# An attention block and two expert layers on one core: the sum's transpose one unit later, the value product in one burst, half of the first weights' low parts on VectorE

## The chip, the cores and the metric

The kernel runs on one core of one Trainium2 chip. The metric is the device time of one execution in microseconds (us). Three runs of the kernel before took 1083.71 us in the median (1083.61 to 1087.17). The engines are TensorE (PE in the profile, PEld for its weight loads), VectorE (DVE), ScalarE (ACT), GpSimd (POOL) and SyncE (SP), which issues most of the DMAs.

## The reference

Three layers follow one another. The whole work is in float32.

```
scores = scale * q @ k.T + bias            # (4 batches, 8 heads, 576, 576); bias = relu(psi w1 + b1) w2, from positions
attn   = exp(scores - max); attn /= sum    # softmax over the last axis
x      = attn @ v                          # -> 2304 tokens x 512
h      = x @ w_in                          # 512 -> 2048
x      = (P(h) / Q(h)) @ w_out             # rational function, 2048 -> 512
h      = max(x @ w1, x @ w2, x @ w3)       # 512 -> 768
out    = h @ w_out2                        # 768 -> 512
```

## The kernel before

**Precision.** A float32 operand of a large product is split into a high part (a rounded cast) and a low part (the rest), and three products of such parts are summed. For the weights of the first expert layer (`wi`, sixteen tiles of 128x512) ScalarE casts the high part (L407) and GpSimd subtracts to get the low part (L408). Which engine subtracts is chosen by `low_eng` from a key of the table `KN`: `LOI` 0 means GpSimd for all of `wi`. The weights come as 64-bit values; ScalarE and VectorE narrow them (L382, L383, L391) in small steps `p1` and `p2` between ticks 9 and 70 of the attention, and SP stores and reloads them.

**Attention.** The work is cut into 80 units: a batch, a pair of heads `p`, and a block `t` of 128 query rows (`t` = 4 has 64 rows of both heads). From the second half of the first batch on, a pair of heads is two groups: rows blocks 0 and 1 (call the units A0, A1), then 2, 3 and 4 (B0, B1, B2). `attn_tick(n)` does for unit n the scores on TensorE (`sc`), the subtraction of the minimum with bias on VectorE (`r0`, `r1`, one for each head, L258) and the exponential on ScalarE (`e0`, `e1`). The sum of the exponentials comes with them. For unit n-1 it does `normalise` (`n`): GpSimd adds a small constant, VectorE takes the reciprocal (L270), GpSimd spreads it to a 128x128 tile `rb` (L272). For unit n-2 it does `T`: TensorE transposes the exponentials in eight pieces into two PSUM banks `tp`, then the last 128 columns into the left part of a bank `tt` (L302), then `rb` into its right part (L303). `v0` and `v1` copy the `tp` banks to `at` (on ScalarE; the second in turn on VectorE and ScalarE) and the whole `tt` to `att` (two of three times VectorE, else ScalarE).

**Value product.** When the last unit of a group has been transposed, `av` multiplies the transposed weights with the values (L338), in pieces over the next ticks: a group of two units takes 3 and 2 of its five column blocks `j`, a group of three 2, 2 and 1. One piece is taken in each tick. When the last is done, `st` multiplies by the transposed reciprocal (L344, VectorE) and SP stores the result.

**Order.** The steps stand in the list `A1` for the first 8 ticks, in `A2` after. In the ticks 8 to 79 the queues of SP, TensorE and VectorE follow the list; a planner at build time orders ScalarE and GpSimd. PSUM has eight banks: two pairs (`wide`, two buffers) for the scores and four single ones (`bank`) for `tp`, `tt`, `av` and others. From tick 61 on `weights_tick` runs at the end of each tick: load, narrow and split, one stage per tick and weight.

**The end of attention.** After unit 79 the ticks 80 to 84 still run `T` and the pieces of `av`, and with each of them one `ffn_tick` of the first expert layer, all in the planner's order on all engines but SP. From `ffn_tick` 5 on every engine follows the list order. An `ffn_tick` is twelve products for `ph`, twelve for `y` and the rational function on VectorE and ScalarE.

Of the kernel before, what the change touches and what calls it, by code (L numbers as in the profile page):

```python
# [17 lines left out]
P = 128  # L18
# [8 lines left out]
HID = 32  # L27
TOFF = 572
TW = 1148
KN = {'NSLOT': 35, 'NRAW': 3, 'NRAWX': 2, 'NATT': 4, 'HB': 0, 'NE': 'd', 'FP': 2, 'BL': 4, 'T4': 0, 'LSP': 1, 'KX': 4, 'HT': 'ss', 'EVP': 'da', 'TTP': 'dda', 'NXS': 4, 'EARLY': 0, 'NM0': 8, 'MAN': 2, 'MANF': 3, 'A1': ['b', 'T', 'sc', 'st', 'r0', 'av', 'b', 'b', 'b', 'sq', 'n', 'r1', 'p2', 'v0', 'v1', 'e0', 'e1'], 'A2': ['sc', 'av', 'p1', 'T', 'r1', 'r0', 'n', 'st', 'p2', 'sq', 'e0', 'e1', 'v0', 'v1'], 'LL': 10, 'SL': 4, 'LL0': 9, 'SL0': 4, 'SQ': [2, 1, 1], 'CUT2': 2, 'CUT3': 3, 'WS': 9, 'WE': 70, 'WT': 61, 'XT': 8, 'XA': 3, 'XB': 8, 'F': ['g2a', 'g2d', 'h', 'g1a', 'w', 'g2p', 'g1d', 'g1p', 'y', 'x', 'g3'], 'LOW': 4, 'LOM': 3, 'LOI': 0, 'GHI': 'dve', 'GLO': 'dve', 'BED': 8, 'BE0': 16, 'NU1': 'pool', 'XE': ['act', 'pool'], 'WR': 1, 'YSP': 'act', 'LAG': 2, 'EV1': 'dve', 'XSE': 'act', 'STQ': 'sp', 'PUQ': 'sp', 'NB0': 0, 'HP': 0, 'SB': 2, 'XLA': 3, 'XLB': 6, 'XSA': 11, 'YL': 10, 'YS': 14, 'WLOW': 1}  # L30
REBIAS = 2.0 ** -112
TOSIGN = -2.0 ** 32
QC = 1.0 + 1e-6
# [4 lines left out]
def tile_attention_moe(  # L38
# [7 lines left out]
    pe, act, dve, pool, sp = nc.tensor, nc.scalar, nc.vector, nc.gpsimd, nc.sync  # L46
# [17 lines left out]
    def big(name, shape, dt=F32):  # L64
        return sb.tile(shape, dt, tag="big", name=name, bufs=2)
# [4 lines left out]
    def bank(name):  # L70
        return ps.tile([P, 512], F32, tag="bank", name=name, bufs=4)
# [25 lines left out]
    A0, A1, A2, A3 = (par[:, i:i + 1] for i in range(4))  # L97
# [65 lines left out]
    def bias_hidden(t, g):  # L163
        hs = []
        for c in range(4):
            if c % 2 == 0:
                ht = {"r": raw, "x": rawx, "s": slot, "b": lambda *a: big(*a)}[KN["HT"][c // 2]](f"h{t}_{g}_{c}", [P, 2, S], F32)
            i0 = t * P + g * 16 + c * 4
# [110 lines left out]
    at = {}  # L279
# [4 lines left out]
        for n, t in enumerate(ts):  # L284
            at[b, t, p] = a, a2, n * P

    def transposes(b, t, p):
        et, st = ex.pop((b, t, p))
        a, a2, off = at[b, t, p]
        nu = 2 if t < 4 else 1  # L290
        flat = et.rearrange("p u j -> p (u j)")
        evac = []
        for u in range(nu):
            tp = bank(f"tp{b}_{t}_{p}_{u}")
            for j in range(4):
                pe.transpose(tp[:, j * P:(j + 1) * P], flat[:, 640 * u + j * P:640 * u + (j + 1) * P], ident)  # L296
            if t < 4:
                evac.append((a[:, :, u, off:off + P], tp.rearrange("p (j i) -> p j i", j=4)))
            else:
                evac.append((a[:, :, :, off:off + 64], tp.rearrange("p (j u i) -> p j u i", j=4, u=2)))  # L300
        tt = bank(f"tt{b}_{t}_{p}")
        pe.transpose(tt[:, :P], flat[:, 512:640], ident)  # L302
        pe.transpose(tt[:, P:2 * P], rbs.pop((b, t, p)).rearrange("p u d -> p (u d)"), ident)  # L303
        tr = tt[:, :2 * P].rearrange("p (w i) -> p w i", w=2)
        if t < 4:
            evac.append((a2[:, :, off:off + P], tr))
        else:
            for u in range(2):
                r = slice(64 * u, 64 * u + 64)
                evac.append((a2[r, :, off:off + 64], tr[r, :, r]))  # L310
        return evac

    def evac(e, pair):
        if e == "a":
            act.copy(*pair)
        elif e == "d":
            dve.tensor_copy(*pair)
        else:
            pool.tensor_copy(*pair)
# [257 lines left out]
    units = []  # L577
# [9 lines left out]
    NU = len(units)  # L587
# [117 lines left out]
    avq, stq = [], []  # L705
# [8 lines left out]
    def attn_tick(n):  # L714
        for t, p in bloads_at.get(n, []):
            if (t, p) not in bias:
                bias_load(t, p)
        for b, p in loads_at.get(n, []):
            if p % 2 == 0:
                load_v(b, p)  # L720
            load_kq(b, p)
        u0 = units[n] if n < NU else None
        u1 = units[n - 1] if 1 <= n <= NU else None
        u2 = units[n - KN["LAG"]] if KN["LAG"] <= n < NU + KN["LAG"] else None
        ev = []
        for step in KN["A1" if n < KN["NM0"] else "A2"]:
            if step == "sc" and u0:
                if u0[2] == u0[1][0]:
                    at_tiles(u0[0], u0[1], u0[3])
                scores(u0[0], u0[2], u0[3])  # L730
            elif step in ("r0", "r1") and u0:
                reduce_min(u0[0], u0[2], u0[3], int(step[1]))
            elif step in ("e0", "e1") and u0 and (step == "e0" or u0[2] < 4):
                expo(u0[0], u0[2], u0[3], int(step[1]))
            elif step == "st":
                while stq:
                    attn_store(*stq.pop(0))
            elif step == "T" and u2:
                ev = transposes(u2[0], u2[2], u2[3])
            elif step == "n" and u1:  # L740
                normalise(u1[0], u1[2], u1[3])
            elif step == "v0" and u2:
                act.copy(*ev[0])  # L743
            elif step == "v1" and u2:
                for e_ in ev[1:len(ev) - 1]:
                    evac(KN["EVP"][n % len(KN["EVP"])], e_)
                evac(KN["TTP"][n % len(KN["TTP"])], ev[-1])
            elif step == "b":
                bias_step()
            elif step in ("p1", "p2"):  # L750
                early_pop(n, 0.5 * int(step[1]))
            elif step == "av":
                if avq:
                    av, js = avq.pop(0)
                    attn_v(*av, js)
                    if 4 in js:
                        stq.append(av)
                if u2 and u2[2] == u2[1][-1]:
                    av = (u2[0], u2[1], u2[3])
                    cuts = {1: (5,), 2: (3, 2), 3: (2, 2, 1)}  # L760
                    cut = {1: (5,), 2: cuts[KN["CUT2"]], 3: cuts[KN["CUT3"]]}[len(u2[1])]
                    avq.extend((av, range(sum(cut[:k]), sum(cut[:k + 1]))) for k in range(len(cut)))
            elif step == "sq":
                for bp in splits_at.get(n, []):
                    sqq.extend(split_kq(*bp))
                for _ in range(2 if n < 10 else KN["SQ"][n % len(KN["SQ"])]):
                    if sqq:
                        sqq.pop(0)()
        WT, XT = KN["WT"], KN["XT"]
        if n == WT:  # L770
            todo.extend((slim["wi"], "wi", f, True, low_eng(KN["LOI"], f)) for f in range(NF))
        if n >= WT:
            weights_tick(KN["WR"])
        if n == NU - XT:
            load_x("x", x_d, 0, 0)
            load_x("x", x_d, 0, 1)
            todo.extend(wo_todo(f) for f in range(NF))
        for m, kcs in ((KN["XA"], (0, 1)), (KN["XB"], (2, 3))):
            if n == NU - XT + m:
                for kc in kcs:  # L780
                    split_x("x", 0, kc)
# [8 lines left out]
        for n in range(KN["NM0"], NU):  # L790
            attn_tick(n)
    n = NU
    while avq or stq or n < NU + KN['LAG']:
        attn_tick(n)
        ffn_tick(n - NU)
        n += 1
# [93 lines left out]
```

## Time and profile before

| | |
|---|---|
| median of three runs | 1083.71 us |
| the profiled execution | 1085.02 us |
| its span, first to last instruction | 1083.2 us |
| TensorE busy, mean granted clock | 1034.7 us (96%), 0.982 |
| VectorE / ScalarE / GpSimd busy | 657.7 / 622.8 / 452.7 us |
| scores, value product, transposes of `e` (L233, L338, L296) on TensorE | 86.4, 79.0 + 23.8, 81.5 us |

Busy time of TensorE is modelled at its ends and consecutive matmuls overlap, so a busy TensorE is read by its successive starts. The attention takes about the first 363 us; the first expert layer follows up to about 780 us, the second to the end. "Granted clock" 1.00 is TensorE's full speed (2.4 GHz), 0.5 its lower level (1.2 GHz).

### The profile page before, as it was taken

To read this page: it belongs to the slowest core of one execution; us is meant where nothing else is said; L and a number is where in the kernel's file an instruction comes from. 1 tells how busy PE (TensorE), PEld (TensorE's weight loads), DVE (VectorE), ACT (ScalarE), POOL (GpSimd) and SP (SyncE) were. 2 spreads that over 40 slices of the span, in tenths; PEclk is the share of its full clock that TensorE was granted. 3 is DMA by queue.
4 is the path that set the end of the run, shared out by engine and by line. 5 is a ranking of instruction groups with operands and counts; after the bars stand their busy time and mean duration, and the time that the engine had idled before them with its cause. 6 is when DMAs were issued, how large, how long until landed. Compare 5 with 4: busy or idle time off the path is not lost. (4 is left out here: it accounts for less than half of the span.)

```text
span 1083.2 us, 16519 instructions
## 1 busy us (share of the span) xinstructions
PE 1034.7 (96%) x5996; PEld 814.2 (75%) x5996; DVE 657.7 (61%) x1296; ACT 622.8 (57%) x1226; POOL 452.7 (42%) x569
## 2 busy tenths in 40 slices
PE   5689899999998889999999999999999999999998
PEld 2247777777765668878889888788888888888887
DVE  8485667676665789777779877799954211111111
ACT  5685676776776878676678766788733211211111
POOL 7605767677696534332233322333533330211111
PEclk9799999999998889999999999999999999999999
DMA  7486854454453442010020200034243200201010
GB/s 266 138 298 216 294 182 151 158 190 158 157 184 123 147 142 78 1 59 1 0 79 1 79 1 0 24 114 136 84 142 105 78 1 1 78 1 59 1 40 20
DMA packets 43394, 107.94 MB, mean 100 GB/s; under 512 B 4784, under 2 KB 11184, under 8 KB 43312
## 3 DMA queue, kind: packets, MB, share of 16 engines
q1 hardware_dynamic: 38128, 96.27, 26.8%
q10 hardware_dynamic: 5184, 10.62, 2.5%
q8 instruction: 47, 0.77, 0.3%
q14 instruction: 35, 0.29, 0.1%
HBM read 77.90 MB, written 28.97 MB: 99 GB/s over the span
## 5 line engine op out<-in xcount | busy, mean ns | idle before, releaser
L454 PE MATMUL p<-ys,wm 128*128 128x512 f32 (+1 forms) x1080 | 227.0, 368 | 0.0
L454 PE MATMUL ph<-xs,wwi 128*128 128x512 f32 (+1 forms) x960 | 215.9, 373 | 3.5 <-ACT at L743 2.6
L454 PEld LDWEIGHTS p<-ys,wm 128*128 128x128 f32 x1080 | 188.9, 188 | 34.3
L454 PE MATMUL y<-gs,wwo 128*128 128x512 f32 (+1 forms) x905 | 204.4, 373 | 1.3 <-POOL gs L502 1.1
L454 PEld LDWEIGHTS ph<-xs,wwi 128*128 128x128 f32 x960 | 169.7, 190 | 38.4 <-POOL xs L446 3.0
L502 POOL TENSOR_TENSOR gs<-g,gs 128x512 fp32r<-128x512 f32 (+1 forms) x80 | 96.1, 1201 | 237.2 <-ACT gs L501 170.2
L454 PEld LDWEIGHTS y<-gs,wwo 128*128 128x128 f32 x905 | 158.4, 188 | 34.5 <-POOL gs L502 2.4
L264 ACT ACTIVATE e<-e,st 128x576 f32<-128x576 f32 x144 | 111.1, 772 | 61.2 <-DVE st L258 44.3
L258 DVE CUSTOM_DVE_ANT_0 e<-s,bias 128x576 f32<-128x576 f32 x144 | 104.3, 754 | 44.9 <-PE s L233 32.4
L546 POOL TENSOR_TENSOR h2s<-mx,h2s 128x512 fp32r<-128x512 f32 (+1 forms) x30 | 35.5, 1183 | 225.5 <-ACT h2s L545 225.5
L542 DVE TENSOR_TENSOR mx<-p,mx 128x512 f32<-128x512 f32 (+1 forms) x30 | 19.1, 637 | 141.4 <-PE p L454 137.5
L475 ACT ACTIVATE s<-ph,keep 128x512 f32<-128x512 f32 (+1 forms) x80 | 49.5, 618 | 90.3 <-PE ph L454 89.9
L545 ACT CAST h2s<-mx 128x512 fp32r<-128x512 f32 (+1 forms) x30 | 17.3, 578 | 127.8 <-DVE mx L543 127.8
L296 PEld LDWEIGHTS tp<-ident,e 128*128 128x128 f32 x576 | 62.1, 141 | 35.7 <-issue 20.1
L233 PE MATMUL s<-k,qs 128*128 128x288 f32 x512 | 86.4, 309 | 2.2 <-ACT bo L194 1.5
L296 PE MATMUL tp<-ident,e 128*128 128x128 f32 x576 | 81.5, 281 | 1.2 <-ACT at L743 1.2
L477 DVE SCALAR_TENSOR_TENSOR g<-g,keep,s 128x512 f32<-128x512 f32 (+1 forms) x80 | 55.3, 692 | 41.5 <-ACT g L476 40.4
L338 PE MATMUL av<-at,v 128*64 128x320 f32 (+3 forms) x576 | 79.0, 396 | 0.0
L560 PE MATMUL o<-wmo,h2s 128*128 128x512 f32 x324 | 78.6, 390 | 0.0
L233 PEld LDWEIGHTS s<-k,qs 128*128 128x128 f32 x512 | 71.3, 191 | 5.6 <-issue 2.6
L185 PE MATMUL pb<-h,keep 128*32 128x288 f32 x576 | 49.2, 450 | 24.1 <-ACT h L173 23.2
L560 PEld LDWEIGHTS o<-wmo,h2s 128*128 128x128 f32 x324 | 60.4, 188 | 12.6 <-POOL h2s L546 0.4
(98 smaller groups left out, 1599.6 us busy)
## 6 DMA issues: line engine op xcount, KB each, us to landing
bias_d<-bo ACTq DMA_DIRECT2D x36, 288.0 KB, 3.1
kr<-in_k SPq DMA_DIRECT2D x16, 576.0 KB, 4.3
qr<-in_q SPq DMA_DIRECT2D x16, 576.0 KB, 4.3
bias<-bias_d SPq DMA_DIRECT2D x16, 576.0 KB, 5.5
wrm<-in_m SPq DMA_DIRECT2D x18, 512.0 KB, 3.6
wrwin<-in_wi SPq DMA_DIRECT2D x16, 512.0 KB, 5.4
wrwo<-in_wo SPq DMA_DIRECT2D x16, 512.0 KB, 3.6
v<-in_v SPq DMA_DIRECT2D x8, 576.0 KB, 4.3
```

The source lines that it names most:

```text
L185: pe.matmul(pb[32 * c:32 * c + 32, x, :HS], lhsT=hw_sb, rhs=hs[c][:, x * HS:(x + 1) * HS], start=True, stop=True,)
L233: pe.matmul(pt[:, x, :HS], lhsT=qs[:, u, t * P:(t + 1) * P], rhs=ks[u][:, w, x * HS:(x + 1) * HS], start=w == 0, stop=w == 1,)
L258: dve.tensor_tensor_reduce(out=dst, in0=src, in1=bs, op0=ALU.add, op1=ALU.min, scale=-0.125, scalar=3.0e38, accum_out=st[:, u:u + 1],)
L264: act.activation(et[:, u], et[:, u], AF.Exp, bias=st[:, u:u + 1], scale=-1.0, accum_out=st[:, 2 + u:3 + u])
L296: pe.transpose(tp[:, j * P:(j + 1) * P], flat[:, 640 * u + j * P:640 * u + (j + 1) * P], ident)
L338: pe.matmul(po[r, :n], lhsT=l, rhs=m, start=j == 0, stop=j == 4, skip_group_check=True)
L454: pe.matmul(po, lhsT=wpart(key, a, k), rhs=rhs, start=first and i == 0, stop=last and i == 2)
L475: act.activation(s, ph, AF.Abs, scale=B0)
L477: dve.scalar_tensor_tensor(q, q, B1, s, ALU.mult, ALU.add)
L502: pool.tensor_tensor(t[1], u, f32(t[0]), ALU.subtract)
L546: pool.tensor_tensor(t[:, 1], m, f32(t[:, 0]), ALU.subtract)
L560: pe.matmul(po, lhsT=h[:, a, tt * P:(tt + 1) * P], rhs=w[c], start=j == 0 and i == 0, stop=j == NF2 - 1 and i == 2,)
```

## The change

The table entries, the order lists and four places in the code change:

```diff
- 'A1': ['b', 'T', 'sc', 'st', 'r0', 'av', ...
+ 'A1': ['b', 'rb', 'T', 'sc', 'rv', 'st', 'r0', 'av', ...
- 'A2': ['sc', 'av', 'p1', 'T', 'r1', 'r0', 'n', 'st', 'p2', 'sq', 'e0', 'e1', 'v0', 'v1']
+ 'A2': ['sc', 'rb', 'av', 'p1', 'T', 'r0', 'r1', 'n', 'rv', 'st', 'p2', 'sq', 'e0', 'e1', 'v0', 'v1']
- 'CUT2': 2, 'CUT3': 3,   'LOI': 0
+                         'LOI': 2
-        tt = bank(f"tt{b}_{t}_{p}")
         pe.transpose(tt[:, :P], flat[:, 512:640], ident)
-        pe.transpose(tt[:, P:2 * P], rbs.pop((b, t, p)).rearrange("p u d -> p (u d)"), ident)
-        tr = tt[:, :2 * P].rearrange("p (w i) -> p w i", w=2)
...
+        evac.append(rows(b, t, p, 0, tt[:, :P]))
+    def rows(b, t, p, w, tr):
+        _, a2, off = at[b, t, p]
+        if t < 4:
+            return [(a2[:, w, off:off + P], tr)]
+        return [(a2[r, w, off:off + 64], tr[r, r]) for r in (slice(0, 64), slice(64, P))]
+    def transpose_sum(b, t, p, tt):
         pe.transpose(tt[:, P:2 * P], rbs.pop((b, t, p)).rearrange("p u d -> p (u d)"), ident)
+        return rows(b, t, p, 1, tt[:, P:2 * P])
...
+        u3 = units[n - KN["LAG"] - 1] if KN["LAG"] < n <= NU + KN["LAG"] else None
+            elif step == "rb" and (u2 or u3):
+                tt = bank(f"tt{n}")
+                if u3:
+                    sums = transpose_sum(u3[0], u3[2], u3[3], tt)
+            elif step == "rv" and u3:
+                for e_ in sums:
+                    evac("d", e_)
             elif step == "T" and u2:
-                ev = transposes(u2[0], u2[2], u2[3])
+                ev = transposes(u2[0], u2[2], u2[3], tt)
...
-                    av = (u2[0], u2[1], u2[3])
-                    cuts = {1: (5,), 2: (3, 2), 3: (2, 2, 1)}
-                    cut = {1: (5,), 2: cuts[KN["CUT2"]], 3: cuts[KN["CUT3"]]}[len(u2[1])]
-                    avq.extend((av, range(sum(cut[:k]), sum(cut[:k + 1]))) for k in range(len(cut)))
+                    avq.append(((u2[0], u2[1], u2[3]), range(5)))
...
-    while avq or stq or n < NU + KN['LAG']:
+    while avq or stq or n <= NU + KN['LAG']:
```

`rb` is transposed for unit n-3, right behind the scores of unit n, into the right part of a bank `tt` that is taken anew in each tick; the left part of the same bank takes the last columns of unit n-2 in `T`. The two parts are copied apart: the sums by `rv` on VectorE, behind `n`, the columns in `v1` as before. `av` of a group runs whole in the tick after its last `T`. `r0` stands ahead of `r1`. With `LOI` 2, `low_eng` gives the odd ones of the sixteen `wi` tiles to VectorE. The attention ends with tick 82 in place of 84, so `ffn_tick` 3 and 4 leave the planned part.

## Rows read from the trace of the kernel before

**Rows 1.** Busy us of each engine, granted clock (PEclk), DMA in stages of 100 us.
```profile
200.00:300.00 100.00, 99.98 (x738) 74.33 (x737) 69.74 (x195) 72.28 (x170) 70.84 (x129) 1.00 0.51 169
300.00:400.00 100.00, 87.88 (x520) 63.17 (x520) 67.27 (x151) 74.28 (x159) 66.57 (x89) 0.90 0.51 157
```
**Rows 2.** What TensorE waited for: us in total, times, longest us.
```profile
PE tt L303 <- POOL rb L272: 8.8, 4, 4.7
PE y L454 <- ACT gs L501: 2.8, 1, 2.8
PE ph L454 <- ACT at L743: 2.6, 1, 2.6
```
**Rows 3.** Stages of 10 us, columns as in Rows 1: PE, PEld, DVE, ACT, POOL, clock.
```profile
320.00:330.00 10.00, 5.32 (x41) 3.67 (x38) 3.83 (x13) 5.98 (x16) 9.61 (x16) 0.91 0.24 69
330.00:340.00 10.00, 10.00 (x58) 7.17 (x57) 4.49 (x13) 5.33 (x14) 5.09 (x9) 0.75 0.57 184
370.00:380.00 10.00, 9.82 (x37) 6.18 (x38) 8.78 (x15) 7.46 (x15) 3.08 (x3) 0.70 0.52 166
390.00:400.00 10.00, 9.96 (x30) 7.56 (x31) 7.79 (x13) 6.95 (x12) 5.29 (x4) 0.68 0.48 164
```
**Rows 4.** Around the longest of those waits, in order of time: start us, us, engine.
```profile
323.83 0.16 DVE L270 RECIPROCAL st<-st 128x1 f32<-128x1 f32 x1 [2.94 <-POOL st L269]
...
329.36 0.29 POOL L272 COPY rb<-st 128x128 f32<-128x128 f32 x1
```
**Rows 5.** GpSimd's low parts of the first weights: busy, mean ns, idle before.
```profile
L408 POOL TENSOR_TENSOR wwi<-wrwi,wwi 128x512 fp32r<-128x512 f32 x15 | 19.3, 1291 | 6.9 <-ACT wwi L407 6.8
```
**Rows 6.** TensorE in order of time, an undisturbed stretch: start us, us.
```profile
335.72 1.29 PE L233 MATMUL s<-k,qs 128*128 128x288 f32 x8
336.94 1.30 PE L338 MATMUL av<-at,v 128*64 128x320 f32 x8
338.17 1.10 PE L296 MATMUL tp<-ident,e 128*128 128x128 f32 x8
...
339.24 1.53 PE L243 MATMUL s<-k,qtail 128*128 128x512 f32 x8
340.70 0.76 PE L338 MATMUL av<-att,v 64*64 64x320 f32 x4
341.39 1.09 PE L296 MATMUL tp<-ident,e 128*128 128x128 f32 x8
```
**Rows 7.** The value product of a group of two: in pieces, and once whole.
```profile
343.69 1.51 PE L338 MATMUL av<-at,v 128*64 128x256 f32 x12
...
347.43 0.65 PE L338 MATMUL av<-at,v 128*64 128x256 f32 x4
...
359.66 1.95 PE L338 MATMUL av<-at,v 128*64 128x256 f32 x16
```
**Rows 8.** VectorE in order of time: the two reductions of one unit.
```profile
337.05 0.76 DVE L258 CUSTOM_DVE_ANT_0 e<-s,bias 128x576 f32<-128x576 f32 x1 [0.24 <-PE s L233]
...
337.73 0.75 DVE L258 CUSTOM_DVE_ANT_0 e<-s,bias 128x576 f32<-128x576 f32 x1
```
**Rows 9.** VectorE by line and shape: busy us, mean ns, idle before.
```profile
L317 DVE COPY at<-tp 128x512 f32<-128x512 f32 x32 | 22.0, 687 | 12.0 <-PE tp L296 11.4
L317 DVE COPY att<-tt 128x256 f32<-128x256 f32 x42 | 17.6, 419 | 17.7 <-PE tt L303 17.6
...
L383 DVE TENSOR_SCALAR wrwin<-wrwin 128x512 int32<-128x512 int32 x16 | 13.0, 813 | 0.0
...
L344 DVE TENSOR_TENSOR xs<-av,att 128x320 f32<-128x320 f32 x14 | 6.6, 472 | 0.0
L408 DVE TENSOR_TENSOR wm<-wrm,wm 128x512 fp32r<-128x512 f32 x6 | 6.5, 1086 | 1.9 <-ACT wm L407 1.9
...
L317 DVE COPY att<-tt 64x128 f32<-64x128 f32 x19 | 5.5, 288 | 7.6 <-ACT att L315 5.0 <-PE tt L303 2.0
...
L408 DVE TENSOR_TENSOR wwo<-wrwo,wwo 128x512 fp32r<-128x512 f32 x4 | 2.7, 681 | 0.0
```

More of the change, by code (lines that the diff above doesn't have):

```diff
@@ L29 @@
 TW = 1148
-KN = {'NSLOT': 35, 'NRAW': 3, 'NRAWX': 2, 'NATT': 4, 'HB': 0, 'NE': 'd', 'FP': 2, 'BL': 4, 'T4': 0, 'LSP': 1, 'KX': 4, 'HT': 'ss', 'EVP': 'da', 'TTP': 'dda', 'NXS': 4, 'EARLY': 0, 'NM0': 8, 'MAN': 2, 'MANF': 3, 'A1': ['b', 'T', 'sc', 'st', 'r0', 'av', 'b', 'b', 'b', 'sq', 'n', 'r1', 'p2', 'v0', 'v1', 'e0', 'e1'], 'A2': ['sc', 'av', 'p1', 'T', 'r1', 'r0', 'n', 'st', 'p2', 'sq', 'e0', 'e1', 'v0', 'v1'], 'LL': 10, 'SL': 4, 'LL0': 9, 'SL0': 4, 'SQ': [2, 1, 1], 'CUT2': 2, 'CUT3': 3, 'WS': 9, 'WE': 70, 'WT': 61, 'XT': 8, 'XA': 3, 'XB': 8, 'F': ['g2a', 'g2d', 'h', 'g1a', 'w', 'g2p', 'g1d', 'g1p', 'y', 'x', 'g3'], 'LOW': 4, 'LOM': 3, 'LOI': 0, 'GHI': 'dve', 'GLO': 'dve', 'BED': 8, 'BE0': 16, 'NU1': 'pool', 'XE': ['act', 'pool'], 'WR': 1, 'YSP': 'act', 'LAG': 2, 'EV1': 'dve', 'XSE': 'act', 'STQ': 'sp', 'PUQ': 'sp', 'NB0': 0, 'HP': 0, 'SB': 2, 'XLA': 3, 'XLB': 6, 'XSA': 11, 'YL': 10, 'YS': 14, 'WLOW': 1}
+KN = {'NSLOT': 35, 'NRAW': 3, 'NRAWX': 2, 'NATT': 4, 'HB': 0, 'NE': 'd', 'FP': 2, 'BL': 4, 'T4': 0, 'LSP': 1, 'KX': 4, 'HT': 'ss', 'EVP': 'da', 'TTP': 'dda', 'NXS': 4, 'EARLY': 0, 'NM0': 8, 'MAN': 2, 'MANF': 3, 'A1': ['b', 'rb', 'T', 'sc', 'rv', 'st', 'r0', 'av', 'b', 'b', 'b', 'sq', 'n', 'r1', 'p2', 'v0', 'v1', 'e0', 'e1'], 'A2': ['sc', 'rb', 'av', 'p1', 'T', 'r0', 'r1', 'n', 'rv', 'st', 'p2', 'sq', 'e0', 'e1', 'v0', 'v1'], 'LL': 10, 'SL': 4, 'LL0': 9, 'SL0': 4, 'SQ': [2, 1, 1], 'WS': 9, 'WE': 70, 'WT': 61, 'XT': 8, 'XA': 3, 'XB': 8, 'F': ['g2a', 'g2d', 'h', 'g1a', 'w', 'g2p', 'g1d', 'g1p', 'y', 'x', 'g3'], 'LOW': 4, 'LOM': 3, 'LOI': 2, 'GHI': 'dve', 'GLO': 'dve', 'BED': 8, 'BE0': 16, 'NU1': 'pool', 'XE': ['act', 'pool'], 'WR': 1, 'YSP': 'act', 'LAG': 2, 'EV1': 'dve', 'XSE': 'act', 'STQ': 'sp', 'PUQ': 'sp', 'NB0': 0, 'HP': 0, 'SB': 2, 'XLA': 3, 'XLB': 6, 'XSA': 11, 'YL': 10, 'YS': 14, 'WLOW': 1}
 REBIAS = 2.0 ** -112
@@ L285, in at_tiles, with transposes @@
             at[b, t, p] = a, a2, n * P
-    def transposes(b, t, p):
+    def transposes(b, t, p, tt):
         et, st = ex.pop((b, t, p))
@@ L300, in transposes @@
                 evac.append((a[:, :, :, off:off + 64], tp.rearrange("p (j u i) -> p j u i", j=4, u=2)))
-        tt = bank(f"tt{b}_{t}_{p}")
         pe.transpose(tt[:, :P], flat[:, 512:640], ident)
-        pe.transpose(tt[:, P:2 * P], rbs.pop((b, t, p)).rearrange("p u d -> p (u d)"), ident)
-        tr = tt[:, :2 * P].rearrange("p (w i) -> p w i", w=2)
[L305 to L311, printed above, removed]
+        evac.append(rows(b, t, p, 0, tt[:, :P]))
+        return evac
+    def rows(b, t, p, w, tr):
[4 more added lines that the diff above has]
+    def transpose_sum(b, t, p, tt):
+        pe.transpose(tt[:, P:2 * P], rbs.pop((b, t, p)).rearrange("p u d -> p (u d)"), ident)
+        return rows(b, t, p, 1, tt[:, P:2 * P])
     def evac(e, pair):
@@ L746, in attn_tick @@
                     evac(KN["EVP"][n % len(KN["EVP"])], e_)
-                evac(KN["TTP"][n % len(KN["TTP"])], ev[-1])
+                for e_ in ev[-1]:
+                    evac(KN["TTP"][n % len(KN["TTP"])], e_)
             elif step == "b":
```

## The prediction

> **What bounds the kernel now.** I read the stages first. Between 200 and 300 us TensorE has no idle time at full clock while the other three engines stand near 70% [rows 1]: the steady attention is bound by TensorE, and so is nearly all behind 400 us, which the change does not touch. Between 300 and 400 us TensorE is busy only 87.9 us and the clock is 0.90 [rows 1]. That is where time can be won. The waits of TensorE say what is late there [rows 2]: the transpose of `rb` waited four times for GpSimd's `rb`, 8.8 us in all, the longest 4.7 us; further 2.8 us for `gs` and 2.6 us for a bank that ScalarE empties, both at the passage to the expert layer. The 10 us stages add the clock [rows 3]: behind the longest `rb` wait (320 to 330, TensorE busy 5.3 us) the granted clock is 0.75, between the full and the half level, so 10 us do the work of 7.5. The same follows the other two waits (0.70 and 0.68).
>
> Why `rb` was late: its reciprocal began at 323.83 us, but GpSimd copied it only at 329.36 us [rows 4]. GpSimd had other work queued ahead (busy 9.6 of 10 us in rows 3), low parts of `wi` of 1.29 us each among it [rows 5].
>
> **The change part by part.** The sum is made against the profiled execution, 1085.0 us, which is 1.3 us over the median of the three runs; I take differences from it and apply them to the median, 1083.7.
>
> *The transpose of `rb` later.* No matmul is added or taken away; L303 moves behind the next unit's scores. From start to start scores take 336.94 - 335.72 = 1.22 us [rows 6], and that is all the slack won: the step stands in front of `av`, not behind it. Waits of 4.7 us would shrink to 3.5, those near 1.5 to 0.3. The longest goes only if GpSimd also gets faster, and it does: eight odd `wi` tiles leave it, 8 x 1.29 = 10.3 us [rows 5] between about 300 and 360 us, when GpSimd is nearly full. `r0` ahead of `r1` starts the exponentials about half a score step (0.6 us) earlier too. At stake are 8.8 us of waits and 10 x (1 - 0.75) = 2.5 us of clock, 11.3 in all. I take -10.3, leaving one short wait; bounds -11.3 and, if the longest stays with its slow clock, -4.6 (11.3 less 3.5 + 0.7 + 2.5). What is then late next is the VectorE queue, below.
>
> *The value product in one burst.* TensorE's work hardly changes: for a group of two, 12 + 4 matmuls in 1.51 + 0.65 = 2.16 us become 16 in 1.95 [rows 7]; times 14 such groups 2.9 us, of which part is only the overlap of neighbours. I take -2 (0 to -2.9). What changes is the rhythm. With starts from rows 6: scores 1.22, `T` 339.24 - 338.17 = 1.07 (about 0.6 for t = 4), scores of t = 4 1.46, `av` of three units 2 x 1.23 + 0.69 = 3.15. Before, every tick had one piece and took some 3.4 us. After, by u0 (unit n): A0 1.22 + 1.07 = 2.3 us, A1 1.22 + 0.6 = 1.8, B0 1.22 + 3.15 + 1.07 = 5.4, B1 2.3, B2 about 5.0. The sum is the same; but A0 and A1 together leave VectorE only 4.1 us, since the scores of B0 need the PSUM pair that `r0` of A1 frees.
>
> *VectorE's queue in those two ticks.* `tt` is one tile with two writers now: `T` writes its left part ahead of `rv` in the list. So I take `rv` to be held until `T` has ended, and behind `rv` on VectorE's queue stand `st`, `p2` and `v1`, then the next `r0`, for which TensorE's scores wait. Before, only the copy of `tt` in `v1` was held that way: 42 copies idled 17.6 us behind L303 [rows 9], at no cost, because nothing of that tick stood behind them. From the end of `T` of B2's tick (start of A0's) until `r0` of A1 has ended, VectorE must do: two sum copies, 2 x 0.29 (the 128-element form); one `st`, 0.47; one wide copy in two ticks, 0.69; the columns' copies, 2 x 2/3 x 0.29 = 0.39; one narrowing op, 0.81 (32 of them lie over 61 ticks, so one in two) [rows 9]; three reductions at 337.73 - 337.05 = 0.68 from start to start [rows 8], 2.04; a reciprocal, 0.16 [rows 4]. That is 5.1 us; successive VectorE starts stand about 0.08 closer than durations (0.76 against 0.68 in rows 8), over six other ops -0.5. So 4.6 against 4.1: TensorE waits about 0.5 us in each pair of heads. 14 pairs give +7. Bounds: 0, if TensorE's run-ahead absorbs it, and +17, if a second narrowing op falls into the two ticks (1.2 a pair).
>
> The rows do not show whether a copy of one part of a bank may run while TensorE writes the other part: in every row of L317 both parts were written before. The Trainium skill ("PSUM — Partial Sum Buffer", section "PSUM bank collisions raise a hardware error") says no two engines may touch one bank on the same partitions at once, and that guarding goes by bank and quadrant, not by address. By that rule the copy waits for `T` and the term is +7; if the parts were free of each other, `rv` and `st` would run during `T`, 0.29 + 0.47 + 0.29 us would leave the chain, and the term would be about +1. I take the first because of the order in the list; no row of the kernel before settles it.
>
> *Low parts on VectorE.* Eight subtractions, each 0.68 us (`wwo`) to 1.09 us (`wm`) by the nearest rows [rows 9]; they wait at the end of a tick, in order, for ScalarE's cast, and the next `r0` stands behind them. VectorE is at about 70% there, so most are hidden; in a short tick they are not. I take +2 (a quarter of a microsecond each); bounds 0 and 8 x 1.09 = +8.7. GpSimd's relief is counted above.
>
> *Two copies for one.* 0.42 us becomes 2 x 0.29 on VectorE, and a tick's extra copy is in the chain already; outside the short ticks VectorE's idle 30% hides it. Cost 0; without that cover 80 x 0.16 = 13 us.
>
> *The passage.* Two joint ticks fewer. In a joint tick both `attn_tick` and `ffn_tick` start a weight, so VectorE gets two weights' narrowing beside the rational function; it is 8.8 us busy of 10 at 370 to 380 [rows 3]. With three such ticks in place of five, four weights spread over later ticks. At stake: 2.8 + 2.6 us of waits [rows 2] and the slow clock behind them, 3.0 + 3.2 us [rows 3], 11.6 in all. But the planner orders this part anew, and `tt` of the last unit takes one more bank. I take -2.5; bounds -9, and +6 for one more such wait (2.8 + 3.2).
>
> The extra bank in each tick (`tt` from the start of the tick) costs nothing as long as `av` holds its bank one tick in place of two or three; the first 90 us keep their order but for `rb` and `rv` and I count them 0 (3 us either way).
>
> **Sum:** -10.3 - 2 + 7 + 2 - 2.5 = -5.8 us. The profiled execution would be 1079.2, the median 1078.
>
> **The rivals.**
> 1. *VectorE becomes the bound in the short ticks: slower.* Place: `r0` of A1 behind `rv`, `st`, `p2`, `v1`. For it: the 4.6 against 4.1 us above has no slack, and the burst holds `st` back to its end. Against it: VectorE is idle 30% of the stage, and late work can be caught up during the next burst. It decides from about 5.3 us in the two ticks on. Price: 1.2 x 14 = 17, low parts +3, against -12.3: +7.7, 1091 us.
> 2. *`rb` stays late: no change.* For it: the slack is only 1.22 us, and the planner may put `rb` behind other work again. Against it: 10.3 us leave GpSimd. -4.6 - 2 + 7 + 2 - 1.5 = +0.9, 1084.6 us.
> 3. *`rv` is not held, and the passage loses one of its waits: clearly faster.* For it: the three quarters of the passage's loss come from two single waits. Against it: the order T before `rv`. -10.3 - 2 + 1 + 2 - 6 = -15.3, 1068 us.
>
> **How the numbers follow.** Chances: forecast 0.42, rival 1 0.20, rival 2 0.22, rival 3 0.16. The forecast's own range is 1072 to 1084. About 0.5% (5.4 us) is what a measurement of this kernel can tell from no change. The forecast lies near that edge: two thirds of it count as faster, one third as the same; rival 2 is the same but for a quarter that is slower. Faster 0.28 + 0.16 = 0.44, same 0.14 + 0.165 + a little of rival 1 = 0.32, slower 0.24. The range from 1066 to 1091 takes in rival 3 and rival 1 at its price, and leaves out their tails.
>
> **What would show it.** Right: the line of L303 waiting for `rb` gone or under 2 us, the clock 1.00 between 310 and 350 us; scores (L233) waiting for VectorE's L258 some 0.3 to 0.6 us in each pair, in the tick behind A1; the copy of the sums idle behind `T`'s L302, not behind L303; eight low parts on VectorE. Wrong: L303 still waiting over 3 us (rival 2); waits of the scores of over 1 us a pair, or VectorE over 80% busy between 200 and 300 us (rival 1); sum copies that start while `T` runs, or a passage without a wait over 1 us (rival 3). The forecast fails if the stage from 130 to 300 us grows by more than about 12 us.

## The result and the profile after

The changed kernel takes 1098.13 us in the median of four runs (1097.78 to 1099.05); the kernel before, run beside it, 1085.44 (1083.61 to 1087.6). The ratio is 1.012, 95% interval 1.0103 to 1.0138: slower by 1.2%, where 1078 was forecast, and outside the range. The profiled execution took 1097.78 us, its span is 1096.0 us, 12.8 longer than before.

The stages of the changed kernel: busy us of TensorE, its weight loads, VectorE, ScalarE and GpSimd, each with its instructions, then the granted clock and the DMA share.

```profile
200.00:300.00 100.00, 94.91 (x690) 70.94 (x689) 68.78 (x212) 65.52 (x153) 68.00 (x123) 1.00 0.44 144
300.00:400.00 100.00, 85.20 (x553) 60.78 (x552) 72.77 (x190) 70.81 (x158) 58.86 (x91) 0.97 0.46 146
...
320.00:330.00 10.00, 8.45 (x58) 5.80 (x59) 7.68 (x24) 7.26 (x18) 6.78 (x13) 1.00 0.70 235
330.00:340.00 10.00, 8.65 (x63) 6.31 (x60) 7.06 (x16) 6.35 (x14) 9.46 (x14) 1.00 0.47 137
370.00:380.00 10.00, 8.26 (x53) 5.95 (x53) 6.67 (x20) 7.27 (x15) 2.64 (x8) 0.91 0.56 171
...
390.00:400.00 10.00, 8.22 (x40) 5.43 (x39) 8.27 (x15) 6.88 (x12) 4.27 (x3) 0.91 0.36 113
```

Against [rows 1, 3] two things changed sides. Between 320 and 340 us the hole is gone (TensorE 5.3 busy us became 8.5, the clock of 0.75 became 1.00). But between 200 and 300 us, where TensorE had no idle time at all, it is now busy 94.9 of 100 us at the same clock, and no other engine is busier than 71 of 100.

What TensorE waited for, changed kernel, whole span, the bias at the start left out (22.8 us, 23.2 before); us in total, times, longest:

```profile
PE s L233 <- DVE st L258: 12.8, 15, 1.8
PE tt L313 <- POOL rb L272: 3.3, 3, 1.8
PE ph L457 <- DVE att L320: 3.0, 1, 3.0
PE tt L313 <- ACT at L754: 2.1, 2, 1.7
PE s L243 <- DVE st L258: 2.1, 6, 0.8
PE av L341 <- DVE g L494: 1.8, 1, 1.8
```

Against [rows 2], the waits for `rb` went from 8.8 to 3.3 us. The new first line is the scores, which wait for VectorE's reductions: 12.8 + 2.1 us in 21 waits.

**Where the 12.8 us lie.** One set of scores (L243) belongs to `t` = 4 and comes once in a pair of heads, so its successive starts measure the pair. From it comes a table with every run below: until the start of the third such scores ("start"); eight steady pairs, from the fourth (142.34 us before, 143.55 after) to the twelfth (278.96 and 290.24); the other five pairs from the third to the sixteenth scores; the passage from there to the first matmul of the second expert layer (tile `p`, 777.46 and 789.81 us). What follows took 305.7 to 307.4 us in every run.

| kernel | start | 8 steady pairs | each | 5 other pairs | passage |
|---|---|---|---|---|---|
| before | 125.1 | 136.6 | 17.08 | 94.6 | 421.2 |
| changed | 125.1 | 146.7 | 18.34 | 98.1 | 420.0 |
| burst alone | 122.4 | 144.1 | 18.01 | 97.9 | 417.9 |
| later transpose alone | 128.2 | 139.5 | 17.44 | 92.5 | 422.9 |
| low parts alone | 124.9 | 136.8 | 17.10 | 91.5 | 423.2 |
| `r0` first alone | 126.5 | 136.3 | 17.03 | 95.1 | 419.2 |
| changed, pieces again | 125.8 | 139.0 | 17.37 | 90.5 | 420.7 |
| changed, sums in scores' banks | 124.4 | 145.3 | 18.16 | 93.2 | 418.3 |
| the same, pieces again | 126.5 | 137.0 | 17.12 | 89.9 | 419.8 |
| changed, no narrowing in short ticks | 133.8 | 141.4 | 17.68 | 93.8 | 423.1 |
| changed, `T` behind `rv` | 128.2 | 154.1 | 19.27 | 100.2 | 418.4 |
| changed, all low parts on GpSimd | 124.8 | 146.8 | 18.34 | 97.4 | 421.5 |
| changed, `r1` first | 125.3 | 147.9 | 18.49 | 99.4 | 422.9 |
| changed, the add on VectorE | 126.7 | 148.2 | 18.53 | 97.3 | 424.8 |
| sums in scores' banks, `st` last | 124.1 | 144.4 | 18.05 | 97.9 | 422.3 |
| low parts and the add on VectorE | 122.4 | 136.4 | 17.05 | 91.4 | 420.8 |
| the same, `r0` first | 121.3 | 136.3 | 17.03 | 91.1 | 421.4 |

Each row is one traced execution. Those of the later transpose alone (1092.27 us) and of the low parts alone (1084.08 us) lie 3.9 and 3.5 us above the median of their runs, so a few microseconds in the start or the passage can be the execution's and not the edit's. The steady pair is firmer: the six kernels without a burst and without a shared bank lie between 17.03 and 17.12.

So the changed kernel loses 10.1 us in the eight steady pairs and 3.5 in the other five, wins 1.2 in the passage, and loses 0.4 behind it. In the steady pairs the parts add up: +7.44 (burst), +2.86 (later transpose), +0.14 (low parts) and -0.35 (`r0` first) make +10.09.

**One pair, read closely.** TensorE and then VectorE in the changed kernel, in order of time (start us, us, what the idle time before it waited for):

```profile
184.43 0.27 PE L301 MATMUL tt<-ident,e 128*128 128x128 f32 x1
184.46 1.30 PE L233 MATMUL s<-k,qs 128*128 128x288 f32 x8
...
188.28 0.27 PE L301 MATMUL tt<-ident,e 128*128 128x128 f32 x1
190.32 1.47 PE L233 MATMUL s<-k,qs 128*128 128x288 f32 x8 [1.77 <-DVE st L258]
191.83 2.38 PE L341 MATMUL av<-at,v 128*64 128x320 f32 x16
```

```profile
184.74 0.29 DVE L320 COPY att<-tt 128x128 f32<-128x128 f32 x1 [1.59 <-PE tt L301]
185.06 0.42 DVE L347 TENSOR_TENSOR xs<-av,att 128x256 f32<-128x256 f32 x1
185.41 0.75 DVE L258 CUSTOM_DVE_ANT_0 e<-s,bias 128x576 f32<-128x576 f32 x1
186.08 0.75 DVE L258 CUSTOM_DVE_ANT_0 e<-s,bias 128x576 f32<-128x576 f32 x1
...
187.63 0.16 DVE L270 RECIPROCAL st<-st 128x1 f32<-128x1 f32 x1 [0.80 <-POOL st L269]
187.72 0.27 DVE L320 COPY att<-tt 128x128 f32<-128x128 f32 x1
187.90 0.91 DVE L386 TENSOR_SCALAR wrwin<-wrwin 128x512 int32<-128x512 int32 x1
188.73 0.67 DVE L320 COPY at<-tp 128x512 f32<-128x512 f32 x1
189.32 0.27 DVE L320 COPY att<-tt 128x128 f32<-128x128 f32 x1
189.52 0.74 DVE L258 CUSTOM_DVE_ANT_0 e<-s,bias 128x576 f32<-128x576 f32 x1
```

The first matmul shown ends the `T` of B2, the second begins A0. A0 and A1 together take TensorE about 4.1 us (184.43 to 188.55). VectorE's queue over the same stretch is the one that the prediction listed: sum copy, `st`, two reductions, reciprocal, copies, a narrowing op, the reduction that frees the PSUM pair. It needs until 190.26, 5.8 us, and TensorE idles 1.77. VectorE itself had stood idle 1.59 us right before, because its next instruction, the sum copy, waited for `T`.

### The profile page after: what moved, and what is told of

Its sections match the earlier page's. It is cut to its first block, busy times and chain, and to the rows that moved or that the text cites. A ratio compares the mean times of both kernels' runs of the same rounds, so it can differ in the third digit from the quotient of the medians.

```text
span 1096.0 us, 16555 instructions
## 1 busy us (share of the span) xinstructions
PE 1034.6 (94%) x5996; PEld 815.6 (74%) x5996; DVE 678.3 (62%) x1403; ACT 622.2 (57%) x1223; POOL 442.7 (40%) x561
## 5 line engine op out<-in xcount | busy, mean ns | idle before, releaser
L233 PE MATMUL s<-k,qs 128*128 128x288 f32 x512 | 88.8, 312 | 14.6 <-DVE st L258 12.8
L296 PEld LDWEIGHTS tp<-ident,e 128*128 128x128 f32 x576 | 63.2, 140 | 19.6 <-issue 12.7
L320 DVE COPY att<-tt 128x128 f32<-128x128 f32 (+1 forms) x160 | 39.6, 258 | 59.4 <-PE tt L301 58.7
L341 PE MATMUL av<-at,v 128*64 128x320 f32 (+3 forms) x576 | 71.8, 386 | 2.8 <-DVE g L494 1.8
L754 ACT COPY at<-tp 128x512 f32<-128x512 f32 x80 | 46.6, 583 | 44.4 <-PE tp L296 44.3
```

The source lines that it names most:

```text
L233: pe.matmul(pt[:, x, :HS], lhsT=qs[:, u, t * P:(t + 1) * P], rhs=ks[u][:, w, x * HS:(x + 1) * HS], start=w == 0, stop=w == 1,)
L341: pe.matmul(po[r, :n], lhsT=l, rhs=m, start=j == 0, stop=j == 4, skip_group_check=True)
```

## The experiments

Each ratio is to the kernel before, run beside it, with its 95% interval. The order lists are cut to what changes.

**The three parts alone.** From the kernel before:

```diff
 burst alone:            -'CUT2': 2, 'CUT3': 3     +'CUT2': 1, 'CUT3': 1
 later transpose alone:  -['sc', 'av', 'p1', 'T', 'r1', 'r0', 'n', 'st', ...]
                         +['sc', 'rb', 'av', 'p1', 'T', 'r1', 'r0', 'n', 'rv', 'st', ...]   and its functions
 low parts alone:        -'LOI': 0                 +'LOI': 2
```

> The kernel before with the value product of a group in one burst and nothing else changed. Theory (VectorE's queue: the copy of the sums is held to the end of T and everything behind it delays the next reductions): here VectorE holds nothing behind T but the copies of v1, so the pair of heads stays near 17.0 us and the time within 3 us of before. Rival A (the burst alone makes the two ticks without a value product too short for VectorE): the pair grows by 0.8 us or more, waits of the scores for L258 as after, time 10 us or more above before.

> The kernel before with the transpose of the sum one unit later alone (value product still in pieces, r1 ahead of r0, all low parts on GpSimd). Theory: the copy of the sums waits for T here too, but each tick keeps some 3.4 us, so the reductions come in time: scores wait under 3 us in all, rb waits 8.8 us go to 2 to 5 us, time 4 to 9 us below before. Rival B (the two copies and the hold cost in every tick): pair period up by 0.5 us or more, time 5 us or more above before.

> The kernel before with half the low parts of wi on VectorE alone. Theory: GpSimd is relieved by some 10 us in the ticks where rb was late, so the two rb waits of 6.3 us between 300 and 330 us and the slow clock behind them (2.5 us) mostly go: 3 to 8 us below before. Rival C (the low parts hold up VectorE's queue behind ScalarE's cast): pairs between 290 and 350 us longer than 18 us through waits of the scores for L258, time equal to before or above.

Measured: burst alone 1090.33 us, 1.0058 [1.0039, 1.0077]; later transpose alone 1088.34, 1.0027 [1.0014, 1.004]; low parts alone 1080.53, 0.997 [0.9958, 0.9983]. Only the low parts are a gain. The later transpose, which was to bring the largest one, costs 3.2 us, where theory had a gain of 4 to 9: in its trace, an execution above the median, 0.36 in each steady pair, 3.1 in the start and 1.7 in the passage, against 2.1 gained in the other five pairs. The burst costs 0.93 us in each steady pair with no later transpose and no `rv` beside it. That is rival A's pair, but half of its 10 us and not by its wait.

There the wait has another name. The kernel with the burst alone, what TensorE waited for in the whole span:

```profile
PE tt L303 <- POOL rb L272: 15.5, 14, 3.0
PE s L233 <- DVE st L258: 2.7, 11, 0.5
```

One pair of it, VectorE, GpSimd and TensorE:

```profile
179.88 0.17 DVE L270 RECIPROCAL st<-st 128x2 f32<-128x2 f32 x1 [0.20 <-POOL st L269]
...
182.64 0.76 DVE L258 CUSTOM_DVE_ANT_0 e<-s,bias 128x576 f32<-128x576 f32 x1 [1.86 <-PE s L233]
```

```profile
179.93 2.53 POOL L141 TENSOR_TENSOR qs<-qr,qs 64x512 fp32r<-64x512 f32 x2
182.53 1.42 POOL L147 TENSOR_TENSOR k<-kr,k 128x576 fp32r<-128x576 f32 x1
183.89 0.29 POOL L272 COPY rb<-st 128x128 f32<-128x128 f32 x1
```

```profile
184.23 0.33 PE L303 MATMUL tt<-ident,rb 128*128 128x128 f32 x1 [0.65 <-POOL rb L272]
...
186.73 1.47 PE L233 MATMUL s<-k,qs 128*128 128x288 f32 x8 [0.45 <-DVE st L258]
```

VectorE starves for scores during the burst and the `T` behind it (1.86 us idle), and later the scores wait 0.45 us for its reductions. But the larger wait, 0.65 us, is for `rb`, and VectorE does not cause it: its reciprocal had ended at 180.05 us, and GpSimd first worked off low parts of `q` and `k`, 4.0 us, before it copied `rb` at 183.89. So it goes in all ten waits of L303 between 130 and 300 us, one in each pair and 9.1 us in all: the reciprocal had ended 3.8 to 5.0 us before the copy, with such low parts between them. These waits are about the whole 0.93 us. In the short ticks the burst alone thus runs into GpSimd's queue, the changed kernel into VectorE's. The short ticks are the same, and the later transpose did take the first chain away (15.5 us to 3.3). That the parts add up in the steady pairs is therefore partly chance: one wait goes and another of its size takes its place.

**Is it the shared bank, or the burst?** First `T` was put behind `rv` and `st` in the changed kernel, so that VectorE is not held; then the pieces came back:

```diff
-'A2': ['sc', 'rb', 'av', 'p1', 'T', 'r0', 'r1', 'n', 'rv', 'st', 'p2', ...]
+'A2': ['sc', 'rb', 'av', 'p1', 'r0', 'r1', 'n', 'rv', 'st', 'T', 'p2', ...]
```

```diff
-                    avq.append(((u2[0], u2[1], u2[3]), range(5)))
+                    av = (u2[0], u2[1], u2[3])
+                    cut = {1: (5,), 2: (3, 2), 3: (2, 2, 1)}[len(u2[1])]
+                    avq.extend((av, range(sum(cut[:k]), sum(cut[:k + 1]))) for k in range(len(cut)))
```

> The changed kernel with T behind rv and st in the list, so that the copy of the sums and the store no longer wait for the end of T (the transposes of T's columns wait for the copy instead); the order on each engine's queue in the steady part is else the same. Theory: the copies of the sums no longer idle behind T's L301 (39 us between 130 and 300 us), the scores' waits for L258 fall from 15 us to under 6, pair period 17.3 to 17.7 us, time 6 to 12 us below the changed kernel. Rival A: the hold does not matter, pair period stays at 18.2 us, time within 3 us of the changed kernel.

> The changed kernel with the value product in pieces again (3 and 2; 2, 2 and 1). The single parts gave +5.2 us (burst), +3.2 (later) and -4.6 (low parts), 3.8 together, against 12.7 for the whole. Theory (the copy of the sums held to the end of T harms only where ticks are short, so burst and later transpose cost more together than alone): pair period back to 17.0 to 17.4 us, scores wait for L258 under 3 us in all, 1080 to 1087 us. Rival D (the rest comes from the low parts on VectorE behind the hold, with or without burst): pairs between 290 and 350 us stay at 19 us or more, 1091 us or more.

Measured: `T` behind `rv` 1109.08 us, 1.0226 [1.0203, 1.025], a pair 19.27 us, slower still, against theory and rival. Pieces again 1084.58, 1.0006 [0.9995, 1.0018]: the burst is worth 13.5 us of the changed kernel by the medians, 12.4 by the two ratios. With `T` behind `rv` the waits pass to TensorE (whole span):

```profile
PE tt L301 <- DVE att L320: 33.2, 42, 3.2
```

In the changed kernel it is VectorE that waits; between 130 and 300 us:

```profile
DVE att L320 <- PE tt L301: 39.2, 19, 2.9
DVE st L270 <- POOL st L269: 9.2, 17, 0.9
```

In these two kernels the program's waits keep the two parts of `tt` apart, whichever engine comes first: the copy of the right part waits for the write of the left one, or the write for the copy. The Trainium skill ("PSUM — Partial Sum Buffer", section "PSUM bank collisions raise a hardware error") says that guarding goes by bank and quadrant and not by address; both traces agree, 39.2 us in 19 waits and 33.2 in 42. What would happen without the waits no run shows.

**The bank taken out.** The sum's transpose goes into unused columns of the scores' own PSUM pair, so `T` has `tt` alone; run with the burst and with pieces:

```diff
+                    dst = sps[u0[0], u0[2], u0[3], int(u0[2] < 4)][:, 1, HS:HS + P] if in_scores else tt[:, P:2 * P]
-                    sums = transpose_sum(u3[0], u3[2], u3[3], tt)
+                    sums = transpose_sum(u3[0], u3[2], u3[3], dst)
```

> The changed kernel with the sum's transpose written into unused columns of the scores' PSUM pair instead of the bank that T writes, so that its copy waits for neither T nor makes T wait; burst, order and low parts as in the changed kernel. Theory: copies of the sums idle under 8 us behind T between 130 and 300 us (39 us before), pair period 17.3 to 17.7 us, 7 to 11 us below the changed kernel. Rival A (the short ticks of the burst are too short for VectorE whatever the hold): pair period 18.0 us or more, within 3 us of the changed kernel.

> The same with the value product in pieces: sum's transpose one unit later in the scores' PSUM pair, low parts half on VectorE. Theory: no hold, no short ticks, so TensorE waits only for rb now and then: pair period 17.0 to 17.2 us also between 290 and 350 us, 3 to 8 us below before. Rival E (the second copy itself costs): pair period 17.4 us or more, equal to before.

Measured: burst 1091.32 us, 1.0067 [1.0046, 1.0088]; pieces 1081.36, 0.9974 [0.9957, 0.9991]. VectorE's waits between 130 and 300 us and then TensorE's in the whole span, kernel with the burst:

```profile
DVE xs L347 <- PE av L341: 21.8, 16, 3.2
...
DVE att L320 <- PE tt L301: 3.2, 5, 0.7
```

```profile
PE s L233 <- DVE att L320: 9.0, 19, 1.5
PE s L233 <- DVE st L258: 6.5, 8, 1.8
```

The 39.2 us of hold are 3.2 now, yet a steady pair only fell from 18.34 to 18.16, which is rival A's pair; the total fell by 6.8 us, near theory's 7, with 4.9 of it in the other five pairs. VectorE idles at the next instruction instead, `st` (L347), which waits for the burst's end. And the edit has a wait of its own, the 9.0 us above: the scores' pair is free only when `rv` has copied the sums out of it, behind both reductions. So with the burst no run shows the price of the hold alone; 0.2 us a pair is what is left after the new wait. With pieces that wait comes five times (4.3 us), never in a steady pair, and a pair goes from 17.37 to 17.12: there the hold costs 0.25 us. The burst costs 0.93, 0.97 and 1.04 us a pair in the three settings, in the first through `rb`, in the other two through VectorE's queue.

**What makes VectorE late in the short ticks?** Three takings-apart: the add of the constant off GpSimd, `st` moved to the end of the tick (on top of the unused columns), and no narrowing in the short ticks:

```diff
 add on VectorE:  -        pool.tensor_scalar(r, r, 1e-9, 0.0, ALU.add, ALU.add)
                  +        dve.tensor_scalar(r, r, 1e-9, 0.0, ALU.add, ALU.add)
 st last:         -'A2': [..., 'n', 'rv', 'st', 'p2', 'sq', 'e0', 'e1', 'v0', 'v1']
                  +'A2': [..., 'n', 'rv', 'p2', 'sq', 'e0', 'e1', 'v0', 'v1', 'st']
 no narrowing:    +                short = n >= KN["NM0"] and u2 and (u2[2] in (3, 4) or u2[2] == 2 and step == "p2")
                  +                if not short:
                       early_pop(n, 0.5 * int(step[1]))
```

> The changed kernel with the small constant added on VectorE, right ahead of the reciprocal, instead of on GpSimd: the reciprocal then waits for no GpSimd instruction. Theory (my chain of VectorE's queue lacked the reciprocal's wait for GpSimd, 9.2 us in 17 waits between 130 and 300 us, which stands between the reductions and the held copies): these waits go, 0.16 us a unit are added, scores' waits for L258 fall from 15 us to 8 to 12, pair period 17.6 to 18.0 us, 3 to 7 us below the changed kernel. Rival F (the reciprocal's wait is covered by the hold that follows it): pair period 18.2 us as before, within 2 us of the changed kernel.

> The kernel with the burst and the sum's transpose in the scores' PSUM pair (1091.3 us, 9.9 us over the same with the product in pieces), with the store's multiplication st moved behind v1, so that VectorE does not stand at the end of the burst with narrowing and copies queued behind it. Theory (the burst costs because in-order VectorE is parked at its end, 21.8 us in 16 waits of st for the product between 130 and 300 us): these waits go, scores' waits for VectorE fall from 15 us to under 8, 3 to 7 us below that kernel. Rival A (two short ticks in a row hold more VectorE work than time, parked or not): within 2 us of it.

> The changed kernel with the narrowing steps kept out of the two short ticks of each pair and out of the step ahead of them (they move to the other ticks, same number). Theory (work queued between the end of T and the second r0 is what TensorE waits for, microsecond by microsecond): about 0.8 us a pair leave that chain, scores' waits for L258 fall from 15 us to 5 to 9, pair period 17.5 to 17.9 us in place of 18.3, 5 to 10 us below the changed kernel. Rival H (the loss does not hang on the length of that chain): pair period 18.1 us or more, within 3 us.

Measured: add on VectorE 1103.83 us, 1.0169 [1.0147, 1.0191]; `st` last 1096.3, 1.0109 [1.0093, 1.0125]; no narrowing 1102.03, 1.0163 [1.0141, 1.0185]. None helps the total (the second goes against 1091.32 us), for three reasons.

The add on VectorE took the reciprocal's wait away (its line of 9.2 us, 17 waits, is gone between 130 and 300 us), but the adds are 80 more instructions in the queue that is late; the scores waited as long:

```profile
PE s L233 <- DVE st L258: 13.7, 17, 1.4
```

With `st` last, VectorE idles at the copies behind `T` instead (130 to 300 us), and the pair is 18.05 where it was 18.16:

```profile
DVE at L320 <- PE tp L296: 14.8, 9, 2.8
DVE att L320 <- PE tt L301: 13.3, 6, 2.9
```

Without narrowing a steady pair is 0.66 us shorter (17.68) and the other five 4.3 in all: 9.5 us less over the 13 pairs. The scores' waits for the reductions fall from 14.9 us to 6.1, one long wait left out. The narrowing is thus part of the late chain, as theory said for the pair. But the start lost 8.7 us and the passage 3.1, so the total rose; the start lost it in one place. TensorE and then VectorE of that kernel:

```profile
130.09 2.29 PE L233 MATMUL s<-k,qs 128*128 128x288 f32 x8 [6.82 <-DVE st L258]
```

```profile
128.94 0.43 DVE L386 TENSOR_SCALAR wrwin<-wrwin 128x512 int32<-128x512 int32 x1 [8.87 <-DMA wrwin<-in_wi]
129.28 0.75 DVE L258 CUSTOM_DVE_ANT_0 e<-s,bias 128x576 f32<-128x576 f32 x1
```

A narrowing op came up in the queue before its weight had landed, VectorE stood 8.87 us at it with the reductions behind, and TensorE 6.82 behind those.

**Low parts and order inside the change.** The changed kernel with all low parts on GpSimd, and with `r1` first; the kernel before with `r0` first:

```diff
 -'LOI': 2    +'LOI': 0
 -[..., 'T', 'r0', 'r1', 'n', ...]    +[..., 'T', 'r1', 'r0', 'n', ...]
 (before)  -[..., 'T', 'r1', 'r0', 'n', ...]    +[..., 'T', 'r0', 'r1', 'n', ...]
```

> The changed kernel with all low parts of wi on GpSimd again. Theory: the surplus lies in burst and later transpose together, so the pairs before 290 us keep 18.2 us; the pairs between 290 and 350 us lose the low parts on VectorE but may wait for rb again: time within 5 us of the changed kernel. Rival D: the pairs between 290 and 350 us fall from 20 to about 18.2 us and the time by 5 us or more.

> The changed kernel with r1 ahead of r0 again, as in the kernel before. Theory: the first reduction then waits for the whole of the scores, and both PSUM pairs come free late: in the short ticks the queue is already late, so little changes: within 3 us of the changed kernel. Rival G (the order of the reductions makes the difference of the burst's cost): 5 us or more to either side.

> The kernel before with r0 ahead of r1 and nothing else. Theory: ticks of 3.4 us hide either order, so TensorE waits as before: within 2 us of before, except for a shift of the rb waits by GpSimd's order. Rival G: 4 us or more to either side.

Measured: all low parts on GpSimd 1099.48 us, 1.0143 [1.0126, 1.0161]; that is 1.4 us over the changed kernel with overlapping intervals, so no gain of the low parts is shown here. `r1` first 1103.77, 1.0168 [1.0144, 1.0192], so `r0` first brings 5.6 where within 3 was expected: 1.2 in the eight steady pairs, 1.3 in the other five, 2.9 in the passage. Alone `r0` first takes 1083.09, 0.9978 [0.9962, 0.9994], about 2. In a steady pair the order is worth 0.15 us in the changed kernel and 0.04 alone (0.35 in eight); why it moves the passage is not shown.

**A faster version.** From the kernel before: low parts on VectorE and the add on VectorE; then `r0` first as well.

```diff
-'LOI': 0    +'LOI': 2
-        pool.tensor_scalar(r, r, 1e-9, 0.0, ALU.add, ALU.add)
+        dve.tensor_scalar(r, r, 1e-9, 0.0, ALU.add, ALU.add)
```

> The kernel before with half the low parts of wi on VectorE and the small constant added on VectorE: GpSimd has two instructions less on the way to rb. Theory: the rb waits that are left with the low parts alone (6.1 us, 5 times) fall under 2 us, with no other wait in their place: 2 to 5 us below that kernel, 5 to 10 us below before. Rival: GpSimd's own order (rb behind the splits of q and k) sets the time of rb, not the add: rb waits stay at 4 us or more, time equal to low parts alone.

> The kernel before with half the low parts of wi and the small constant on VectorE (1077.7 us) and r0 ahead of r1 (2 us below before when alone). If the two are independent: 1075 to 1077 us; if the second was only a shift of GpSimd's order: within 2 us of 1077.7, to either side.

Measured: 1077.72 us, 0.9933 [0.9914, 0.9951], and 1077.67, 0.9941 [0.9923, 0.996]. Both beat both kernels; `r0` first adds nothing on top. What TensorE waited for in the first, whole span:

```profile
PE s L233 <- DVE st L258: 2.9, 3, 2.1
PE tt L303 <- POOL rb L272: 2.2, 2, 1.9
```

The waits for `rb` fell from 8.8 us [rows 2] to 2.2, with the transpose where it was. With the low parts alone they were

```profile
PE tt L303 <- POOL rb L272: 6.1, 5, 2.2
...
PE s L233 <- DVE st L258: 0.6, 2, 0.4
```

The same add that cost time in the changed kernel gains some 3 us here. By the traces the gain is not in the late pairs: the other five take 91.4 us with the add and 91.5 without; a wait of 2.1 us for VectorE's reductions came up there. It lies in the start (2.5 us), where a wait of 2.2 us for `rb` is gone, and in the passage (2.4), which no run explains. That the add is cheap here because the ticks are even is likely but not shown.

## Why the prediction was wrong

**The failed steps.** The forecast was -5.8 us, the result +12.7 against the kernel before beside it. Two steps make up the miss, about equally. The burst stands at -2 and +7 in the sum and cost 13.5. The rest of the change (later transpose -10.3, low parts +2, passage -2.5) stands at -10.8 and was worth nothing clear of noise: 1.0006 with pieces again.

The first is "VectorE's queue in those two ticks", put at 4.6 against 4.1 us, "about 0.5 us in each pair", +7. The place, two short ticks and VectorE's queue in them, was right; the size was not. The burst, which makes those ticks short, costs 0.97 us a pair (changed against pieces again), twice the term and near rival 1's 1.2 a pair. Rival 1, with +17 for this term, came to 1091; the rest of its miss lies in the gains below. In the pair above VectorE needed 5.8 us where 4.6 were listed. The rows give the difference: 0.80 the reciprocal waited for GpSimd, 0.3 from the start of `T`'s last matmul to the copy behind it, 0.1 for a narrowing op of 0.91 in place of 0.81. The sum had added durations as if nothing in the chain waited for another engine. Its range did reach to +17.

**What the term was tied to** was wrong too. The sum took +7 if `rv` is held and about +1 if it is not: the hold was to decide. The hold is there (39.2 us), but without it a pair is only 0.18 us shorter (18.34 to 18.16, the new wait included), and the burst costs as much. What decides is that a burst of some 3 us (191.83 to 194.82) is followed by two ticks of 4.1 us, too short for VectorE's chain of 5.8 us; with the transpose in its old place they are too short for GpSimd's, and a pair takes 18.01 with no `rv` at all. Pieces gave each tick its share. That rules out rival 3.

**The transpose of `rb` later, -10.3**, is the second failed step. The waits went from 8.8 to 3.3 us, just over the 3 that was to speak for rival 2, and the clock was 1.00 from 310 to 350. The gain is smaller. Two of the four waits, 0.95 and 1.52 us at 76 and 117 us, did not lie in the late pairs at all. With pieces again, the five pairs outside the steady stretch take 4.1 us less than before, and 3.7 us more than five of its own steady pairs (17.37), where before it was 9.2: 5.5 of the 10.3 at most. In the changed kernel the same five pairs lose 3.5, since VectorE's queue is late there as well. Most of the gain needed no moved transpose: low parts alone shorten them by 3.1 us, the move alone by 2.1, and the move costs 0.36 in each steady pair, 0.25 of it by the shared bank, for which the sum had nothing.

**The burst saves TensorE 2 us.** Not seen: the matmuls did come in fewer pieces (2.38 us for sixteen at 191.83), but no stage became shorter, as TensorE is no longer what bounds a pair.

**Low parts on VectorE, +2.** They take 7.5 us, 0.94 each, between the ends taken from [rows 9]:

```profile
L411 DVE TENSOR_TENSOR wwi<-wrwi,wwi 128x512 fp32r<-128x512 f32 x8 | 7.5, 939 | 0.0
```

The net of cost and GpSimd's relief is -4.6 us alone and not clear of noise in the changed kernel (-1.4).

**Two copies for one, 0.** Right where it can be told: with both copies, the later transpose, its own bank and pieces a steady pair takes 17.12 us against 17.08.

**The passage, -2.5.** It gave -1.2 (421.2 to 420.0), inside its bounds, and a difference that two executions of one kernel can show as well. The waits did not get shorter: 3.0 us for `att`, 1.8 for `g` and 1.7 for `at` stand where 2.8 and 2.6 us stood. The granted clock of its first 50 us rose from 0.86 to 0.93.

**The tests.** "Waits of the scores of over 1 us a pair" spoke for rival 1: 14.9 us over 14 pairs. "VectorE over 80% busy" did not: it was 69% busy, and that test was wrong in itself, since it idled in the burst and was late in the ticks behind it. The forecast also said that it fails if 130 to 300 us grows by more than about 12. That came up: the ten pairs from the third scores to the thirteenth (125.05 to 295.99 us before, to 310.29 after) grew by 14.3.

**Left open:** why the burst costs 7.6 us in the other five pairs of the changed kernel (98.1 against 90.5) but 3.3 alone (97.9 against 94.6). The start and the passage differ by some 7 us over the table (121.3 to 128.2 but for one kernel, 417.9 to 424.8); with one trace of each kernel, what the edit does there and what the execution does cannot be told apart. With `st` last the total holds a stretch at a clock of 0.78 to 0.88 between 310 and 330 us, behind two waits of 1.8 and 3.1 us; what started it was not followed.

## What to carry to other kernels

An in-order engine that is 70% busy can bound a loop: add up its queue tick by tick, against the shortest ticks and not the mean, and put the waits for other engines inside the chain into the sum. Do it for every engine: here GpSimd's queue was as short of time as VectorE's, and taking its wait away only handed the loss on. Work cut into pieces is worth more than its overhead when the pieces are what keeps the ticks even. Before moving a late step, relieve the engine that makes it late: here that alone was the gain (-4.6 us; the move alone +3.2).

## What the runs showed of the hardware

Two users of different columns of one PSUM bank were kept apart by waits, and the price depended on which one came second (no run lets them overlap): with VectorE second 39.2 us of its time went between 130 and 300 us (36.1 with pieces, where taking it away gave 0.25 us a pair); with TensorE second 33.2 us of its time went in the whole span and a pair grew from 18.34 to 19.27 us. Sums put into columns that the scores leave unused took the first wait down to 3.2 us and used no further bank, but the next scores then waited 9.0 us for their copy.

Half of a small PSUM copy costs two thirds of the whole: 128x256 took 0.419 us [rows 9], 128x128 0.278, and a quarter of that, 64x64, still 0.220:

```profile
L320 DVE COPY att<-tt 128x128 f32<-128x128 f32 x106 | 28.5, 278 | 29.1 <-PE tt L301 28.9
...
L320 DVE COPY att<-tt 64x64 f32<-64x64 f32 x54 | 11.9, 220 | 30.3 <-PE tt L301 29.8
```
